# One-megabyte weight loads issued in four pieces, and a list schedule drawn with other ties

## Chip, cores and metric

One core of a Trainium2 chip runs the whole program. The metric is the device time of one execution in microseconds (us); the number given for a kernel is the median of several runs. The kernel before takes 2373.57 us, the median of 3 runs that lie between 2373.34 and 2375.6 us.

## The reference, cut to what matters

One sequence of 2048 tokens with 1024 features goes through four residual layers, A, B, A, B. Both A layers use the same weights, and so do both B layers.

```python
x = A_x                                               # (1, 2048, 1024) bf16
x = x + A(layernorm(x));  x = x + B(layernorm(x))
x = x + A(layernorm(x));  x = x + B(layernorm(x))

A: q, k, v = x @ wqkv                                 # 32 heads of 32
   phi(t) = [softmax(t @ w_phi), softmax(-t @ w_phi)]
   kv = phi(k).T @ v;  z = sum(phi(k))                # 64 x 32 for each head
   return (phi(q) @ kv / (phi(q) . z + 1e-6)) @ wo    # cost linear in the tokens
B: p = softmax(q @ k.T / sqrt(32))                    # 2048 x 2048 for each head
   return (p @ v) @ wo
```

Layer B holds most of the work: 32 heads times 2048 x 2048 exponentials, twice.

## The kernel before, in words

The residual stream `xT` stays in SBUF with the features on partitions (8 feature blocks of 128). Tokens are handled in four chunks of 512. Everything else that lives in SBUF is cut from one large tile, `arena`, and everything in PSUM from one tile, `psum`, of eight banks; so most rows of the profile name only these two.

**Nothing is issued in the order of the source.** Each helper (`layernorm`, `a_keys`, `a_queries`, `b_k`, `b_v`, `b_o`, `attention`, `slab`, ...) only records operations: an engine, a duration that the planner believes, dependencies, buffers, a priority, and a function that emits the instructions. `Sched.run` (line 152) is a list scheduler. It plays the engines forward in its own time, gives each free engine the ready operation with the lowest priority value whose buffers it can allocate, and places the buffers in the arena at that moment. Its result is one order of operations, emitted as it stands; on the chip every engine then works through its own list in order, with semaphore waits where data come from another engine. A small change of a believed duration can therefore move thousands of instructions, though no instruction is added.

The work falls into five stages:

- **A of layer pair 1**: chunks are normalized, keys and values of A are made (`a_keys`, matmuls at line 480, exponentials at L688, softmax sums L692/L695/L701), then queries (`a_queries`, L814 to L883), and A's projection (L896). TensorE works without a break.
- **B of layer pair 1** (`attention`): for each group of three units TensorE makes a score tile of 128 x 1536 (line 1104, three matmuls of 32 rows that run side by side), ScalarE takes its exponential (L1113), and TensorE multiplies the result by the values and by ones (L1145, four matmuls of 32 columns that run side by side). Some units are left to VectorE, which builds 2^x out of integer and polynomial steps (L1047 to L1061, its scores at L1040). Into the gaps of TensorE go the projections for later head groups and chunks (the same helper as at line 480, but in column quarters, so at line 484) and, where nothing is ready, filler matmuls: at L1377 (zeros added to the open accumulator) or through line 484 with `onesD`. The fillers are there to keep TensorE busy enough; the planner puts one in when less than 75% of the last 3.4 us of its own time was worked (`KEEP`, `SPELL`).
- **The change of layers**: the last chunk's output projection, then A of pair 2 for queries, as above. The keys of A for three of four chunks were already made among B's exponentials (`a_keys(..., alone=True)`, with the evictions at L685), and their normalized chunks were stored to DRAM (`xd`, L1368) and are loaded back (L1262).
- **B of layer pair 2**, and **a short tail** (L1171 to L1182, L1022, L1024).

The denominators of B take a round trip: when both accumulators of a head group are copied out (L1161), four small DMAs bring the sums onto more partitions (L1191), VectorE inverts them (L1196), one DMA writes them to DRAM (`rd`, L1197), one reads them back spread over 128 partitions (L1199), and two multiplications finish the group (L1202). All loads and stores but two are issued by the SP queue, one after the other; SP waits for the arena's space before a load, and all that stands behind a load waits too.

Weights come through `slab(cls, prio, src, n)` (line 582). With n = 512 that is a 1 MB load of 128 partitions x 8 feature blocks x 512: the values' and keys' weights of A (`wv_slab`, `wk_slab`, from A_wqkv and from `wd_k`), those of the queries from `wd_q`, B's value weights (`bv_s`) and B's output weights of the last layer (`bo_s`). With n = 128 it is 256 KB (`w2`, `w2o`). A consumer (`mmg2`, line 738) takes the eight blocks in four steps of two, and waits at step i for entry i of the list that `slab` returns; before the change the list holds the same load four times.

Two constants of the planner matter below: a DMA of kb kilobytes costs it 0.55 us on the issuing queue and 2.0 + kb/200 us until it has landed, and `RING` lets half of the size part of one transfer delay the next.

## Time and profile before

| what | value |
|---|---|
| median of 3 runs | 2373.57 us (2373.34 to 2375.6) |
| the profiled execution's own time | 2381.73 us |
| its span, first to last instruction | 2379.9 us |
| mean granted TensorE clock in it | 0.989 |
| ScalarE busy | 2072.2 us, 87% |
| TensorE busy | 2241.8 us, 94% (fillers among it) |
| VectorE busy | 1669.0 us, 70% |
| SP queue | 112.29 MB, 17.6% of 16 DMA engines' time |

The profile is one execution; the chip's profiler records the start and end of each instruction. "Idle before" a group of instructions is the time that its engine stood still just ahead of it, followed by what ended the wait. A row of a table of stretches gives the stretch, its length, the busy time of each engine with the number of instructions, then the granted clock of TensorE (1.00 is full speed), the busy share of the DMA engines and the GB/s.

### The profile page before, as it was taken

Reading aid. Unit: us, or ns where it says so; the run is one execution under the profiler, and the core shown is the slowest. Engines: PE = TensorE matmul, PEld = TensorE weight load, DVE = VectorE, ACT = ScalarE, POOL = GpSimd, SP = SyncE. Lnnn points to the kernel's source line nnn. Section 1 sums busy time; section 2 is a strip of 40 time slices with the busy share of each in tenths; the row PEclk is TensorE's granted clock in tenths of the full one; section 3 lists DMA queues with packets and bytes.
Section 4 is the critical chain, followed back from the end, with each engine's and each line's share of the span. In section 5 each row is a group of like instructions: output and inputs, shape, how many; then the busy total and the mean of one; then the engine's idle time right before and its main releaser. Section 6 shows DMA issues by size and latency. Waiting matters only on the chain.

```text
span 2379.9 us, 67117 instructions
## 1 busy us (share of the span) xinstructions
PE 2241.8 (94%) x29746; PEld 872.4 (37%) x29816; DVE 1669.0 (70%) x2135; ACT 2072.2 (87%) x1850; POOL 25.2 (1%) x70
## 2 busy tenths in 40 slices
PE   7999999999999999999998999999999999899998
PEld 4443343333333333333333434433333333333333
DVE  7987752345678676764764776489888988977763
ACT  5436559999999999999997555899999999999998
POOL 0000000000000000000000000000000000000000
PEclk9999999999999999999999999999999999999999
DMA  9210101122131222213323001110111101111111
GB/s 213 64 37 1 32 21 36 29 52 53 44 92 54 57 59 68 82 55 86 112 73 108 28 3 34 31 27 25 36 27 31 33 25 29 40 50 44 38 30 35
DMA packets 218092, 118.69 MB, mean 50 GB/s; under 512 B 139208, under 2 KB 208840, under 8 KB 217032
## 3 DMA queue, kind: packets, MB, share of 16 engines
q1 hardware_dynamic: 215720, 112.29, 17.6%
q8 instruction: 233, 3.82, 0.7%
q10 hardware_dynamic: 2080, 2.10, 0.3%
q14 instruction: 59, 0.48, 0.1%
HBM read 78.71 MB, written 14.14 MB: 39 GB/s over the span
## 4 chain that ended last, share of the span: by engine, by line
ACT 26%; PE 16%; issue 6%; DVE 5%; DMA 1%; SPq 0%; ACTq 0%; DVEq 0%; another core or an unknown queue 0%
ACT arena L1113 25%; PE psum L480 8%; PE psum L484 2%; PE psum L1145 2%; PE psum L1104 2%; DVE arena L1058 2%; DVE arena L1061 1%; DMA arena<-rd 1%; DVE arena L1047 1%; DVE arena L1050 0%; ACT arena L688 0%; DVE arena L1202 0%; PE psum L857 0%; PE psum L1377 0%; DVE arena L1161 0%
## 5 line engine op out<-in xcount | busy, mean ns | idle before, releaser
L1113 ACT ACTIVATE arena<-psum 128x1536 bf16<-128x1536 f32 x1295 | 1749.4, 1670 | 20.5 <-PE psum L1104 12.9
L1145 PE MATMUL psum<-arena 128*32 128x512 bf16 x4096 | 626.7, 386 | 12.1 <-DVE arena L1161 7.6
L1145 PE MATMUL psum<-arena,ones_bf 128*32 128x512 bf16 x4096 | 626.6, 386 | 1.3 <-issue 1.3
L484 PE MATMUL psum<-arena 128*32 128x512 bf16 (+1 forms) x9792 | 590.0, 356 | 6.5 <-DVE arena L920 3.0
L1104 PE MATMUL psum<-arena 32*128 32x512 bf16 x3884 | 513.9, 384 | 84.0 <-ACT arena L1113 75.0
L480 PE MATMUL psum<-arena 128*128 128x512 bf16 (+1 forms) x1969 | 446.6, 376 | 10.8 <-DVE arena L1182 3.6
L1058 DVE SCALAR_TENSOR_TENSOR arena<-arena 128x1024 f32<-128x1024 f32 x318 | 387.7, 1219 | 6.3 <-PE psum L1145 2.2
L1104 PEld LDWEIGHTS <-arena 32*128 32x128 bf16 x3884 | 173.7, 91 | 572.5 <-issue 561.4
L484 PEld LDWEIGHTS <-arena 128*32 128x32 bf16 x9792 | 221.6, 96 | 231.0 <-issue 120.0
L480 PEld LDWEIGHTS <-arena 128*128 128x128 bf16 x2032 | 190.6, 98 | 245.6 <-issue 45.9
L1145 PEld LDWEIGHTS <-arena 128*32 128x32 bf16 x4096 | 166.8, 95 | 247.1 <-issue 191.1
L1047 DVE TENSOR_SCALAR arena<-psum 128x512 int32<-128x512 f32 x212 | 145.8, 688 | 80.4 <-PE psum L1040 69.6
L920 DVE CAST arena<-psum 128x512 bf16<-128x512 f32 x120 | 82.5, 687 | 155.7 <-PE psum L484 141.7
L1145 PEld LDWEIGHTS <-ones_bf 128*32 128x32 bf16 x4096 | 163.8, 95 | 30.3 <-issue 15.9
L1061 DVE SCALAR_TENSOR_TENSOR arena<-arena 128x1024 bf16<-128x1024 f32 x106 | 129.3, 1220 | 3.5 <-PE psum L1145 0.2
L688 ACT ACTIVATE arena<-psum 128x512 bf16<-128x512 f32 x80 | 43.0, 597 | 87.5 <-PE psum L480 66.6
L1161 DVE COPY arena<-psum 128x512 f32<-128x512 f32 x126 | 86.4, 686 | 44.1 <-PE psum L1145 43.0
L1377 PE MATMUL psum<-xT,zero 128*32 128x512 bf16 x1360 | 111.5, 384 | 0.0
L1202 DVE TENSOR_TENSOR arena<-arena 64x512 bf16<-64x512 f32 x124 | 84.7, 683 | 34.4 <-DMA arena<-rd 21.0
L692 DVE TENSOR_REDUCE arena<-arena 128x32 f32<-128x1024 bf16 x64 | 77.7, 1214 | 32.5 <-ACT arena L688 31.0
L814 ACT ACTIVATE arena<-psum 128x512 bf16<-128x512 f32 x128 | 69.4, 597 | 31.4 <-PE psum L480 30.6
L572 DVE TENSOR_TENSOR arena<-xT,arena 128x1024 f32<-128x1024 bf16 x64 | 77.8, 1219 | 24.4 <-ACT arena L561 23.8
(102 smaller groups left out, 1359.4 us busy)
## 6 DMA issues: line engine op xcount, KB each, us to landing
arena<-rd SPq DMA_DIRECT2D x62, 256.0 KB
arena<-in_B_wqkv_dram SPq DMA_DIRECT2D x48, 256.0 KB
arena<-in_A_wqkv_dram SPq DMA_DIRECT2D x10, 1024.0 KB
arena<-arena SPq DMA_DIRECT2D x256, 32.0 KB
arena<-in_B_wo_dram SPq DMA_DIRECT2D x32, 256.0 KB
arena<-wd_k SPq DMA_DIRECT2D x8, 1024.0 KB
arena<-arena SPq DMA_DIRECT2D x96, 64.0 KB
arena<-in_B_wqkv_dram SPq DMA_DIRECT2D x4, 1024.0 KB
```

Of the source, the lines that this page charges most:

```text
L480: nc.tensor.matmul(out_, lhsT=lhsT, rhs=rhs, start=start, stop=stop, skip_group_check=True)
L484: nc.tensor.matmul(out_[ks, :], lhsT=lhsT[:, ks], rhs=rhs, start=start, stop=stop, tile_position=(0, 32 * k), skip_group_check=True)
L920: return op("DVE", dve_us(512), lambda: nc.vector.tensor_copy(out=dst(), in_=src()), [dep], bufs, prio)
L1047: ys.append(op("DVE", dve_us(512), lambda k=k, s_v=s_v: nc.vector.tensor_scalar(out=y_v()[:, k, :].bitcast(I32), in0=s_v(), scalar1=POW2_B ...
L1058: last = [op("DVE", dve_us(1024), lambda i=i, c=c: nc.vector.scalar_tensor_tensor(out=x_v(), in0=(x_v() if i else m_v()), scalar=c, in1=m_ ...
L1061: eo = op("DVE", dve_us(1024), lambda: nc.vector.scalar_tensor_tensor(out=e_v(), in0=x_v(), scalar=POW2_0, in1=y_v(), op0=ALU.add, op1=ALU ...
L1104: nc.tensor.matmul(out=s_v()[:, x * C512:(x + 1) * C512], lhsT=kT[g][1]()[r, pp, d * P:(d + 1) * P], rhs=q_of[(qc, g)][1]()[r, (pp + j // ...
L1113: ex = op("ACT", act_us(w * C512), lambda s_v=s_v, e_v=e_v, w=w: nc.scalar.activation(out=e_v()[:, 0:w * C512], in_=s_v(), func=ACT.Exp, s ...
L1145: nc.tensor.matmul(out=a_v()[col:col + 32, :], lhsT=v_v()[:, kc % 4, o:o + DH] if what == 0 else ones_bf[:], rhs=ev()[:, x * C512:(x + 1) ...
L1161: cp = op("DVE", dve_us(512), lambda t_v=t_v, a_v=a_v: nc.vector.tensor_copy(out=t_v(), in_=a_v()), [last], [a_b, t_b], prio - 4)
L1202: s = [op("DVE", dve_us(512), lambda a=a, k=k, o_v=o_v, r_v=r_v, T=T: nc.vector.tensor_tensor(out=o_v()[a, :], in0=T[k][1]()[a, :], in1=r_ ...
L1377: nc.tensor.matmul(psum[32 * k:32 * k + 32, 6 * C512:7 * C512], lhsT=zero[:], rhs=xT[:, 0, 0:C512], start=False, stop=False, tile_position ...
```

## The change

Loads with n = 512 are issued as four DMAs of two feature blocks each (256 KB), and the list that the consumer waits on holds the four pieces. The three loads of normalized chunks at L1262 are cut in the same way. Loads with n = 128, the turned loads of `slab_turned` (L595), the two loads on ScalarE's queue (L603) and the three stores at L1368 stay as they are. And before planning, each believed duration of a VectorE or TensorE operation is multiplied by a random factor between 0.99 and 1.01, drawn with seed 14, so that operations that tied or nearly tied are taken in another order.

```diff
+TIE = 14
 ...
     def run(self):
+        draw = random.Random(TIE)
+        for o in self.ops:
+            if TIE and o.eng in ("DVE", "PE"):
+                o.dur *= 1 + draw.uniform(-0.01, 0.01)
 ...
     def slab(cls, prio, src, n, deps=(), q="SP"):
         b, v = sb(cls, PO, n)
-        o = dma(prio, lambda: (nc.sync if q == "SP" else nc.scalar).dma_start(out=v(), in_=src),
-                deps, [b], q=q, kb=2 * n)
-        return b, v, [o] * 4
+        if n < C512:
+            o = dma(prio, lambda: (nc.sync if q == "SP" else nc.scalar).dma_start(out=v(), in_=src),
+                    deps, [b], q=q, kb=2 * n)
+            return b, v, [o] * 4
+        return b, v, [dma(prio + 0.001 * i, lambda i=i: (nc.sync if q == "SP" else nc.scalar).dma_start(
+            out=v()[:, 2 * i:2 * i + 2, :], in_=src[:, 2 * i:2 * i + 2, :]),
+            deps, [b], q=q, kb=n / 2) for i in range(4)]
 ...
-                xnA[c] = (x_b, x_v, [dma(second - 20 + 20 * c, lambda c=c, x_v=x_v: nc.sync.dma_start(
-                    out=x_v(), in_=xd_v[:, c, :, :]), [xnA[c]], [x_b], kb=1024)] * 4)
+                xnA[c] = (x_b, x_v, [dma(second - 20 + 20 * c + 0.001 * i, lambda c=c, x_v=x_v, i=i: nc.sync.dma_start(
+                    out=x_v()[:, 2 * i:2 * i + 2, :], in_=xd_v[:, c, 2 * i:2 * i + 2, :]),
+                    [xnA[c]], [x_b], kb=256) for i in range(4)])
```

More of the change, by code (lines that the diff above doesn't have):

```diff
@@ L2 @@
 import math
+import random
 from contextlib import ExitStack
```

## Prediction

> **What bounds the kernel now.** I read the busy times by stage first, cut where the first and the last exponential of each attention lie; the first attention begins at 357.5. A row is stretch, length, then PE, PEld, DVE, ACT and POOL busy with their instructions.

> ```profile
> 357.50:1285.00 927.50, 872.26 (x13218) 321.10 (x13219) 557.00 (x705) 911.78 (x712) 11.51 (x24) 0.99 0.23 65
> 1285.00:1499.70 214.70, 209.99 (x1556) 89.67 (x1575) 154.62 (x213) 117.65 (x201) 2.60 (x8) 0.98 0.10 30
> 1499.70:2369.00 869.30, 815.85 (x12020) 305.88 (x12022) 679.75 (x837) 860.78 (x645) 0.00 (x0) 0.99 0.12 33
> ```

> TensorE bounds the change of layers (second row). In the two attentions ScalarE does: it is idle for 927.50 - 911.78 = 15.7 us of the first and 869.30 - 860.78 = 8.5 us of the second. So an order that only moves work inside the attentions can win at most 24 us. Next, the groups by line, to see who waits there:

> ```profile
> L1113 ACT ACTIVATE arena<-psum 128x1536 bf16<-128x1536 f32 x1295 | 1749.4, 1670 | 20.5 <-PE psum L1104 12.9 <-PE psum L484 3.7 <-PE psum L1145 2.8
> ...
> L484 PEld LDWEIGHTS <-arena 128*32 128x32 bf16 x9792 | 221.6, 96 | 231.0 <-issue 120.0 <-DMA arena<-in_B_wqkv_dram 0.8 <-DVE arena L576 0.3
> ```

> The exponentials waited 20.5 us in all, for TensorE. The second row has the largest wait of these projections for a weight load, 0.8 us. Where do the 20.5 us lie? In stretches of 10 us with a low granted clock (third number from the end), one undisturbed stretch first:

> ```profile
> 1020.00:1030.00 10.00, 8.68 (x117) 2.97 (x118) 9.86 (x13) 10.00 (x8) 0.53 (x1) 1.00 0.03 8
> 1090.00:1100.00 10.00, 7.54 (x200) 2.77 (x192) 0.83 (x2) 6.92 (x6) 0.00 (x0) 0.83 0.42 124
> 1180.00:1190.00 10.00, 9.50 (x119) 3.19 (x119) 8.02 (x8) 6.26 (x7) 0.09 (x1) 0.79 0.09 25
> 1210.00:1220.00 10.00, 8.83 (x80) 2.31 (x79) 7.94 (x12) 8.14 (x7) 0.59 (x1) 0.66 0.01 3
> 1270.00:1280.00 10.00, 8.01 (x94) 2.31 (x91) 6.40 (x9) 7.62 (x6) 0.00 (x0) 0.83 0.25 54
> 1700.00:1710.00 10.00, 10.00 (x119) 2.88 (x115) 7.84 (x10) 9.00 (x7) 0.00 (x0) 0.85 0.06 15
> 1750.00:1760.00 10.00, 8.45 (x96) 2.56 (x95) 9.04 (x12) 9.16 (x7) 0.00 (x0) 0.83 0.01 1
> 1810.00:1820.00 10.00, 9.83 (x123) 2.83 (x119) 8.26 (x10) 8.89 (x7) 0.00 (x0) 0.89 0.06 15
> 1970.00:1980.00 10.00, 10.00 (x122) 2.90 (x119) 8.81 (x10) 9.21 (x8) 0.00 (x0) 0.87 0.05 12
> ```

> ScalarE loses 10 minus its fourth busy time: 3.08, 3.74, 1.86, 2.38, then 1.00, 0.84, 1.11 and 0.79 us, 14.8 together. These **falls of the clock** are what an order can change. What comes ahead of one, in single us:

> ```profile
> 1175.00:1176.00 1.00, 0.39 (x3) 0.10 (x3) 1.00 (x2) 1.00 (x1) 0.00 (x0) 1.00 0.33 113
> 1176.00:1177.00 1.00, 0.45 (x4) 0.19 (x4) 1.00 (x3) 1.00 (x2) 0.00 (x0) 1.00 0.09 33
> 1178.00:1179.00 1.00, 1.00 (x11) 0.30 (x12) 0.87 (x2) 1.00 (x2) 0.00 (x0) 0.50 0.05 4
> ```

> Two us with TensorE below half busy, then half clock. Such a gap can be found in the program's order: I counted the matmuls that stand between one score group (L1104 x3) and the next. In five places of the attentions (their starts aside) two neighbouring intervals hold five matmuls or fewer. By the number of the exponential they stand at 486, 589, 801, 880 and 998, and the counts of exponentials up to a time place them (the fourth, 880, lies between the last two rows):

> ```profile
> 0.00:1026.00 1026.00, 658.53 (x487) 1.00 0.23 58
> 0.00:1176.90 1176.90, 797.31 (x589) 1.00 0.24 63
> 0.00:1698.00 1698.00, 1084.13 (x801) 0.99 0.21 56
> 0.00:1968.00 1968.00, 1350.47 (x999) 0.99 0.20 52
> ```

> The last four, where one interval is empty and the other holds five, are each followed by one of the falls above (1180, 1700, 1810, 1970). The first, with four matmuls and then one, is not (1020 to 1030 has clock 1.00). The other four falls do not stand in the order: they come from waits as they happened.

> **The change part by part.** *Loads in pieces.* 26 loads and the three of L1262 become four DMAs each, 87 issues more on SP. An earlier first piece is worth what waits for a load now; that is about 0.8 us by the row above, and taken as 0 (bounds 0 and -0.8). Issues cost most at the start, where SP has no pause:

> ```profile
> 13.82 1.04 SPq L584 DMA_DIRECT2D arena<-in_A_wqkv_dram  x2
> ...
> 37.88 7.66 SPq L515 DMA_TRANSPOSE xT<-in_A_x_dram  x3
> ```

> One issue is 1.04/2 = 0.52 us; six more are 3.1 us. In the new order five transposed loads of x stand behind the second store of `wd_k` and not three; that store waits for VectorE, so they end 2 x 7.66/3 = 5.1 us later, at 45.5 + 5.1 = 50.6 us. The first reader of chunk 2 is

> ```profile
> 54.27 3.71 ACT L538 ACTIVATE arena<-xT 128x2048 bf16<-128x2048 bf16 x2
> ```

> so 3.6 us of cover are left: cost 0, and up to 5.1 us if landing takes longer than that.

> [...]

> *The other order.* Instruction counts stay the same on ScalarE and VectorE; TensorE loses 28 filler groups of L1377 (1360 to 1248 matmuls) and gains one of the other kind. The split alone leaves the second attention's TensorE order untouched; the tie seed moves it. Term by term:

> 1. *Falls.* In the new order the sparse places are 762 (four matmuls, then one, like 486 which did not fall) and 998 (five and none, as before). 589, 801 and 880 are filled. That removes 3.74 + 1.00 + 1.11 = 5.85 us. For 762 I add 0.4 of the mean of the three falls of the second attention, 0.4 x (1.00 + 1.11 + 0.79)/3 = 0.39. Bounds: nothing removed and a fall at 762, +0.97; all gone with 998 too, -6.6.

> [...]

> 2. *Start of the second attention.*

> ```profile
> 1499.76 1.45 ACT L1113 ACTIVATE arena<-psum 128x1536 bf16<-128x1536 f32 x1 [0.95 <-PE psum L1104]
> 1501.11 0.71 ACT L564 ACTIVATE arena<-arena,eps 128x512 f32<-128x512 f32 x1
> 1501.86 0.63 ACT L566 ACTIVATE arena<-arena 128x512 f32<-128x512 f32 x1
> ...
> 1513.55 0.37 ACT L919 CAST arena<-psum 128x256 bf16<-128x256 f32 x1 [0.92 <-PE psum L480]
> ...
> 1516.98 13.54 ACT L1113 ACTIVATE arena<-psum 128x1536 bf16<-128x1536 f32 x10 [1.31 <-PE psum L1104]
> ```

> Today the ninth exponential starts at 1516.98, after evictions that TensorE feeds one by one. In the new order ScalarE does L564, L566 and one eviction (L919) first (1501.11 + 0.71 + 0.63 + 0.37 = 1502.8), then six exponentials, two evictions, two exponentials, two evictions: 8 x 13.54/10 + 0.55 + 3 x 0.37 = 12.5, ninth at 1515.3, with one eviction (0.37) still to come. Gain 1516.98 - 1515.3 - 0.37 = 1.3. Bounds: -3.2 (all waits in these rows), +1.9.

> 3. *End of the first attention.* There VectorE stands in L1202 for a round trip of the denominators:

> ```profile
> 1269.67 1.41 DVE L1202 TENSOR_TENSOR arena<-arena 64x512 bf16<-64x512 f32 x2 [4.37 <-DMA arena<-rd]
> ```
> ```profile
> L990 DVE TENSOR_TENSOR arena<-xT,psum 128x512 f32<-128x512 bf16 x8 | 5.5, 688 | 16.7 <-PE psum L484 16.6
> ```
> ```profile
> 1270.43 2.79 ACT L1113 ACTIVATE arena<-psum 128x1536 bf16<-128x1536 f32 x2 [0.75 <-PE psum L1104]
> 1274.19 1.45 ACT L1113 ACTIVATE arena<-psum 128x1536 bf16<-128x1536 f32 x1 [0.97 <-PE psum L1104]
> 1276.62 8.16 ACT L1113 ACTIVATE arena<-psum 128x1536 bf16<-128x1536 f32 x6 [0.97 <-PE psum L1104]
> ```

> Behind it waits the eviction L990, behind that TensorE (one PSUM bank serves these projections), behind that the scores; ScalarE loses 0.75 + 0.97 + 0.97 = 2.69. In the new order three of the eight L990 stand behind L1202 and not one. I take two L990 more, 2 x 0.69 = +1.4 (the second row gives 688 ns for one). Bounds -2.69 and 4.37 - 0.75 = +3.6.

> 4. *Change of layers and tail*: the same matmuls in a TensorE stage 98% busy (209.99 of 214.70): 0, bounds ±2.

> Sum: -5.85 + 0.39 - 1.3 + 1.4 = -5.4 us. The profiled execution took 2381.73, so 2376.3 in its terms; it lies 8.2 us above the median of the runs, and the same difference taken from the median gives 2373.57 - 5.4 = **2368.2 us**, -0.23%.

> **The rivals.**

> *More falls go than the order shows.* The four that come from waits (3.08, 1.86, 2.38, 0.84) are accidents of one order; should the new one avoid those of 1090 and 1210 as well, it is -5.4 - 4.9: 2363.3 us. For: these waits lie among the keys that are made alone, and every one of those moved. Against: the new order has 28 filler groups fewer to cover gaps.

> *No net gain.* Falls return elsewhere, as five of the former eight places did not follow from the order alone (four waits and the phase of the one that stayed harmless at 486): 2373.6 us.

> *Slower: evictions stuck behind the round trips.* VectorE waited 21.0 us for `rd` in 11 of its L1202 places, and only the one at 1269 reached ScalarE:

> ```profile
> DVE arena L1202 <- DMA arena<-rd: 21.0, 11, 4.4
> ```

> SP now puts four issues where one was, 3 x 0.52 = 1.6 us longer ahead of a round trip's next DMA, and the seed places L1202 anew among the evictions. Each further place that reaches the scores costs what that one does, 2.69 us. It decides from (5.4 + 4.7)/2.69, about four places; with five, 2368.2 + 13.4 = 2381.6 us. Against it: few loads are cut inside the second attention.

> [...]

> *The pieces don't do what they say* (nobody waits for a whole load): already in the sum, at 0.

> **How the numbers follow.** A measurement of this kernel tells about 0.2% (4.7 us) from no change, so faster is below 2368.8 and slower above 2378.3. Chances: the forecast 0.42, its own range 2364 to 2373, 0.28 of it below 2368.8; more falls gone 0.17; no net gain 0.12; late start 0.05, 0.04 of it inside; stuck evictions 0.24. Faster 0.28 + 0.17 = 0.45; same 0.14 + 0.12 + 0.04 = 0.30; slower 0.24 + 0.01 = 0.25. The range of 8 in 10: below, the second case with another 4 us (the remaining accidents): 2359; above, the slower case at five places: 2382.

> **What would show it.** Right: clock 1.00 after exponentials 589, 801 and 880 and a fall after 998; ScalarE idle in the attentions below 20 us; the ninth exponential of the second attention about 15 us after the first scores; ScalarE squaring chunk 2 without a wait for x. Wrong: clock falls at places that the order does not mark; L1202 with long waits for `rd` and idle scores behind it; a wait for DMA on TensorE or ScalarE in the first 60 us.

## The result, and the profile after

The changed kernel takes 2370.64 us, the median of 12 runs (2365.42 to 2376.02), beside 2374.03 us for the kernel before on the same chip (12 runs, 2369.76 to 2378.05). The ratio is 0.9983, with a 95% interval of 0.9976 to 0.9991. On another chip it was run once more (after_again below): 0.9987, 0.9975 to 0.9999. So it is faster by 0.1 to 0.2%, 3 to 4 us. Forecast were 5.4 us.

The profiled execution after took 2372.59 us (span 2370.8), close to its median; that of before, 2381.73, lay 7.7 us above its own. The difference of the two profiles, 9.1 us, is therefore mostly one of two executions. Where a place is compared below, more than one profile of an order is used.

The three stages, cut as in the prediction at the first and the last exponentials (stretch, length, busy PE, PEld, DVE, ACT, POOL, then clock, DMA share, GB/s), and the exponentials' group:

```profile
351.50:1277.05 925.55, 868.82 (x13201) 319.03 (x13201) 556.64 (x705) 915.41 (x716) 12.01 (x24) 0.99 0.24 65
1277.05:1491.30 214.25, 209.56 (x1564) 89.31 (x1587) 156.66 (x216) 118.17 (x203) 2.57 (x8) 0.99 0.11 33
1491.30:2359.70 868.40, 810.49 (x11933) 302.67 (x11935) 677.26 (x833) 858.93 (x643) 0.00 (x0) 0.99 0.12 33
```
```profile
L1123 ACT ACTIVATE arena<-psum 128x1536 bf16<-128x1536 f32 x1295 | 1749.7, 1703 | 18.4 <-PE psum L1155 7.3
```

ScalarE's idle time is 10.1 us in the first attention (925.55 - 915.41) and 9.5 in the second (868.40 - 858.93); before it was 15.7 and 8.5. (The prediction's first row begins at 357.5, but the first exponential of before is at 353.30; ScalarE was busy for all of the 4.2 us between, so the 15.7 us stand, and the row's length is not to be compared.) The exponentials (now line 1123) waited 18.4 us in place of 20.5. The change of layers is 0.45 us shorter.

Now the places that the prediction named. Exponentials 589, 801 and 880 lie in the first, third and fourth row of this table of 10 us stretches, 998 in the last two; row two is where the clock fell before behind 589:

```profile
1170.00:1180.00 10.00, 8.71 (x129) 3.14 (x125) 5.20 (x8) 10.00 (x11) 0.32 (x1) 1.00 0.67 220
1180.00:1190.00 10.00, 9.50 (x145) 3.58 (x143) 5.06 (x7) 10.00 (x10) 0.33 (x1) 1.00 0.72 234
1680.00:1690.00 10.00, 9.12 (x117) 2.90 (x112) 8.87 (x13) 10.00 (x9) 0.00 (x0) 1.00 0.03 5
1790.00:1800.00 10.00, 8.72 (x122) 2.85 (x114) 9.94 (x12) 10.00 (x9) 0.00 (x0) 1.00 0.07 15
1950.00:1960.00 10.00, 8.75 (x111) 2.81 (x107) 9.32 (x13) 10.00 (x8) 0.00 (x0) 0.92 0.07 15
1960.00:1970.00 10.00, 9.81 (x122) 2.89 (x114) 8.07 (x10) 8.89 (x8) 0.00 (x0) 0.91 0.06 15
```

The clock stays at 1.00 where the places were filled, ScalarE is busy for the whole 10 us, and 998 falls, as forecast. What the forecast did not have:

```profile
1080.00:1090.00 10.00, 6.45 (x68) 1.79 (x64) 3.19 (x4) 6.65 (x6) 0.00 (x0) 0.73 0.36 74
1090.00:1100.00 10.00, 9.31 (x237) 3.46 (x229) 1.12 (x2) 8.40 (x7) 0.00 (x0) 0.93 0.33 82
...
1860.00:1870.00 10.00, 8.91 (x138) 3.53 (x138) 8.41 (x10) 9.23 (x7) 0.00 (x0) 0.83 0.01 2
...
2080.00:2090.00 10.00, 9.12 (x115) 2.70 (x118) 9.59 (x13) 7.24 (x6) 0.00 (x0) 0.83 0.01 2
```

ScalarE loses 3.35 and 1.60 us at 1080 to 1100 (3.08 before, at 1090), 0.77 us at 1860, where the clock falls at a place that the forecast's count does not mark, and 2.76 us at 2080, where before had a full stretch:

```profile
2080.00:2090.00 10.00, 8.70 (x119) 3.09 (x112) 9.36 (x13) 10.00 (x9) 0.00 (x0) 1.00 0.82 219
```

The cause at 2080 is read from four views of the same microseconds: VectorE, TensorE and ScalarE with the idle time ahead of each group in brackets, and what SP issued.

```profile
2075.11 1.21 DVE L1071 SCALAR_TENSOR_TENSOR arena<-arena 128x1024 bf16<-128x1024 f32 x1
2079.54 0.68 DVE L1212 TENSOR_TENSOR arena<-arena 64x512 bf16<-64x512 f32 x1 [3.22 <-DMA arena<-rd]
2080.15 0.68 DVE L1057 TENSOR_SCALAR arena<-psum 128x512 int32<-128x512 f32 x1
```
```profile
2080.88 0.40 PE L490 MATMUL psum<-xT,onesD 128*32 128x512 bf16 x4 [2.48 <-DVE arena L1057]
```
```profile
2082.76 2.80 ACT L1123 ACTIVATE arena<-psum 128x1536 bf16<-128x1536 f32 x2 [2.46 <-PE psum L1155]
```
```profile
2068.23 0.34 SPq L1207 DMA_DIRECT2D rd<-arena  x1
2068.61 1.46 SPq L594 DMA_DIRECT2D arena<-in_B_wo_dram  x3
2070.11 2.52 SPq L591 DMA_DIRECT2D arena<-in_B_wqkv_dram  x2
2073.04 1.83 SPq L1209 DMA_DIRECT2D arena<-rd  x1
```

The chain runs upward. SP writes a group's denominators (L1207) and, ahead of reading them back (L1209), issues five loads, three of them pieces. VectorE stands 3.22 us in L1212 until the read has landed. Behind L1212 waits L1057, behind that a filler matmul of TensorE that wants L1057's PSUM bank, and behind the filler the scores: ScalarE loses 2.46 us, and 0.23 more at the half clock that follows. Together 2.69 us, the price that the rival "stuck behind the round trips" was given, at one place.

### The profile page after: what moved, and what is told of

It reads as the page before. It is cut to its first block, busy times and chain, and to the rows that moved or that the text cites. A ratio compares the mean times of both kernels' runs of the same rounds, so it can differ in the third digit from the quotient of the medians.

```text
span 2370.8 us, 67055 instructions
## 1 busy us (share of the span) xinstructions
PE 2228.1 (94%) x29641; PEld 864.8 (36%) x29708; DVE 1668.6 (70%) x2135; ACT 2069.9 (87%) x1850; POOL 25.6 (1%) x70
## 3 DMA queue, kind: packets, MB, share of 16 engines
q10 hardware_dynamic: 2080, 2.10, 0.3%
## 5 line engine op out<-in xcount | busy, mean ns | idle before, releaser
L1123 ACT ACTIVATE arena<-psum 128x1536 bf16<-128x1536 f32 x1295 | 1749.7, 1703 | 18.4 <-PE psum L1155 7.3
L1057 DVE TENSOR_SCALAR arena<-psum 128x512 int32<-128x512 f32 x212 | 145.7, 687 | 82.6 <-PE psum L1050 73.1
L1212 DVE TENSOR_TENSOR arena<-arena 64x512 bf16<-64x512 f32 x124 | 84.7, 683 | 39.2 <-DMA arena<-rd 34.2
L1388 PE MATMUL psum<-xT,zero 128*32 128x512 bf16 x1248 | 102.2, 382 | 0.0
```

The lines of the kernel that those rows point to most:

```text
L1057: ys.append(op("DVE", dve_us(512), lambda k=k, s_v=s_v: nc.vector.tensor_scalar(out=y_v()[:, k, :].bitcast(I32), in0=s_v(), scalar1=POW2_B ...
L1123: ex = op("ACT", act_us(w * C512), lambda s_v=s_v, e_v=e_v, w=w: nc.scalar.activation(out=e_v()[:, 0:w * C512], in_=s_v(), func=ACT.Exp, s ...
L1212: s = [op("DVE", dve_us(512), lambda a=a, k=k, o_v=o_v, r_v=r_v, T=T: nc.vector.tensor_tensor(out=o_v()[a, :], in0=T[k][1]()[a, :], in1=r_ ...
L1388: nc.tensor.matmul(psum[32 * k:32 * k + 32, 6 * C512:7 * C512], lhsT=zero[:], rhs=xT[:, 0, 0:C512], start=False, stop=False, tile_position ...
```

## The experiments

The first four ran together on one chip, the next four on one, the last three on one. The kernel before took 2379.63, 2379.27 and 2378.37 us there, so the ratios are compared, not the times.

**1. The order without the pieces (order_whole).** Every engine but SP keeps the changed kernel's instructions one for one.

```diff
-        lambda i=i: (...).dma_start(out=v()[:, 2 * i:2 * i + 2, :], in_=src[:, 2 * i:2 * i + 2, :])
+        lambda i=i: i == 0 and (...).dma_start(out=v(), in_=src)
```

> The order of the changed kernel on every engine but SP, with each one-megabyte load issued whole where its first piece stood. If the gain comes from the order (my theory), it keeps the gain: 2369 to 2372 us, about 2370.6. If it comes from the pieces (first rival), it is back at 2374. If the pieces cost something because four issues hold up the reads of the denominators behind them (second rival; in the profile after, the reads at 1074 and 2073 stand behind pieces and VectorE waits 3.7 and 3.2 us for them), it is faster than the changed kernel by up to 5 us: 2366.

Measured: 0.9972 (0.9957 to 0.9987). The whole gain is there without a single piece on the chip; what the pieces changed in the plan is still in it, since the order was planned with them. The second rival is not borne out by its own place: with whole loads the waits at the same two round trips remain, 2.45 us of ScalarE's time at 1081 and 2.08 at 2077, and VectorE's sum of waits for `rd` is no smaller. One row of VectorE's waits each (total us, times, longest), of the changed kernel and of this one:

```profile
DVE arena L1212 <- DMA arena<-rd: 34.2, 15, 7.4
```
```profile
DVE arena L1212 <- DMA arena<-rd: 36.0, 16, 7.7
```

**2. The pieces without the order (before_pieces).** The kernel before, each 1 MB load emitted as four DMAs at its place.

```diff
-        o = dma(prio, lambda: (...).dma_start(out=v(), in_=src), deps, [b], q=q, kb=2 * n)
+        o = dma(prio, lambda: [(...).dma_start(out=v()[:, r:r + 2, :], in_=src[:, r:r + 2, :])
+                               for r in range(0, 8, 2)] if n == C512 else ..., deps, [b], q=q, kb=2 * n)
```

> The order of the kernel before on every engine, only the 29 one-megabyte loads issued as four pieces at the place where the whole load stood. If only the order matters: 2374 us, within 2 us of before. If the pieces bring the gain: 2370.6. If the pieces hold up the denominators: above 2375, with more than 21 us of waits for rd at L1202's multiplications.

Measured: 0.9992 (0.9979 to 1.0005): the pieces by themselves change nothing that can be told. This profile is also a second look at the order of before:

```profile
1180.00:1190.00 10.00, 8.90 (x134) 3.28 (x135) 9.17 (x10) 8.62 (x8) 0.00 (x0) 1.00 0.28 79
1690.00:1700.00 10.00, 8.75 (x99) 2.80 (x100) 8.41 (x10) 8.93 (x7) 0.00 (x0) 0.83 0.01 2
1800.00:1810.00 10.00, 8.74 (x99) 2.65 (x100) 9.01 (x11) 8.91 (x7) 0.00 (x0) 0.83 0.06 14
1960.00:1970.00 10.00, 8.69 (x96) 2.49 (x88) 9.32 (x11) 9.22 (x8) 0.00 (x0) 0.83 0.07 16
```
```profile
DVE arena L1204 <- DMA arena<-rd: 32.3, 14, 4.9
```
```profile
56.02 3.71 ACT L538 ACTIVATE arena<-xT 128x2048 bf16<-128x2048 bf16 x2
```

801, 880 and 998 fall again; 589 does not, and costs 1.38 us in place of 3.74. VectorE's waits for `rd` are 11.3 us longer than the 21.0 of before, as the extra issues on SP would have it, and hardly any of that reaches ScalarE. The first reader of x's second chunk is 1.75 us later than the 54.27 of before: with the old order the issues at the start do show, in this one profile. In the new order it begins at 53.70 with pieces (trips_again) and at 53.61 without (order_whole), the clock being full ahead of it in both; so there they cost 0.1 us, in the main as forecast. (54.32 in the changed kernel's own profile stands behind one step of half clock.)

**3. Filling the sparse places (after_dbl).** Where little TensorE work stands between two score groups, the first group is computed again into the same banks, 293 repeats in all.

```diff
-    for o in sch.run():
-        o.fn()
+    plan = sch.run()
 ...                                                    # between: us of TensorE work up to the next score group
+            o.again = 2 if between < 0.3 else 1 if between < 0.55 else 0
+    for o in plan:
+        for _ in range(1 + o.again):
+            o.fn()
```

> The changed kernel, with a score group computed once or twice again (the same values into the same banks) where fewer than 0.55 or 0.3 us of other TensorE work stand before the next score group in the plan. If falls of the clock come from sparse places of the order, those at 1862 and 1958 go and the mean clock rises to 0.995 or more; falls stay only behind waits of 2.5 us and more (1082, 1263, 2080); the time falls by 2 to 4 us, to 2367 to 2369. If such falls cost nothing that is not hidden, it stays at 2370.6. If the repeated scores hold up the exponentials, it is slower than 2372, with more idle time before the exponentials and no fewer falls.

Measured: 1.0001 (0.9989 to 1.0014). The falls at 1862 and 1958 are gone, the clock is 0.996, and the gain with them:

```profile
1950.00:1960.00 10.00, 9.98 (x131) 3.25 (x131) 9.92 (x14) 10.00 (x8) 0.00 (x0) 1.00 0.12 33
1960.00:1970.00 10.00, 9.34 (x128) 2.98 (x125) 8.95 (x11) 10.00 (x9) 0.00 (x0) 1.00 0.05 11
...
1860.00:1870.00 10.00, 9.45 (x122) 3.05 (x123) 9.07 (x12) 10.00 (x8) 0.00 (x0) 1.00 0.21 48
```
```profile
L1125 ACT ACTIVATE arena<-psum 128x1536 bf16<-128x1536 f32 x1295 | 1750.4, 1604 | 23.2 <-PE psum L1115 9.7
```

That fits falls made by sparse places, though it is one profile, and 998 stayed at full clock without any repeats in one of eight (trips_again). The forecast of 2 to 4 us gained failed: the exponentials now wait 23.2 us, 9.7 of them for their scores, in place of 18.4 and 6.3. That the repeats stand in the way of scores that were only just in time fits the row; which of the 293 do it wasn't separated.

**4. Reads of the denominators first (after_rdfirst, after_trips).** The planned order is kept; the loads (the turned ones apart) that SP issues between a group's write L1207 and its read L1209 go behind the read. First in all 62 round trips:

```diff
+    for bk in [o for o in plan if o.back is not None]:      # bk: the read; bk.back: its write
+        lo, hi = plan.index(bk.back), plan.index(bk)
+        late = [o for o in plan[lo + 1:hi] if o.load and not any(x in plan[lo:hi] for x in o.out)]
+        plan[lo + 1:hi + 1] = [o for o in plan[lo + 1:hi + 1] if o not in late] + late
```

> The changed kernel, with the weight loads that SP issues between the write and the read-back of one group's denominators moved behind the read. If those pieces are what makes the read late, the waits at 1082 and 2080 (ScalarE idle 2.5 us each) shrink below 0.5 us and the time falls by 3 to 6 us, to about 2366; the waits of the L1212 multiplications for rd fall from 34 to about 20 us. If the read is late because of transfers already on the queues, nothing changes: 2370.6. If the loads come too late instead, TensorE waits for DMA and it is slower.

Measured: 0.9963 (0.995 to 0.9976). The stall at 1082 is gone, that at 2080 is 1.23 us, but VectorE's sum of waits for `rd` is 32.7 us, not 20. I then took waits of this profile at 400, 818 and 959 for the price of the other moves, and moved loads in two trips alone:

```diff
-    for bk in [o for o in plan if o.back is not None]:
+    for bk in [o for o in plan if o.back is not None][24:52:27]:     # the 25th and the 52nd
```

> The changed kernel; only in the two round trips whose read stood behind loads and held up the scores (the 25th and the 52nd of the 62) the read goes ahead of these loads (four pieces of A's values' weights; three of B's output weights and two small ones). If the read was late because of these loads, ScalarE's 2.5 us at 1082 and 2.5 us at 2080 go, with the half clock behind them (another 1 to 2 us): 4 to 6 us less than the changed kernel beside it, and none of the new waits at 400, 818 and 959 that moving all loads brought. If the read is late without them too, no difference beyond 1 us.

Measured: 0.9960 (0.9948 to 0.9972), and 0.9953 (0.9936 to 0.9969) when it was run again (trips_again). On the chip of after_again it is 6.6 us faster than the changed kernel (2367.96 against 2374.6), and the fastest version of the study that was run twice. In the two profiles the two places account for 3.3 us of that (4.52 to 0.76 us of ScalarE's idle time at the first, 1.29 to 1.73 at the second); where the rest lies is open. Here are SP's queue and VectorE at the 25th trip, the changed kernel first, then this one (its line numbers lie one to eight further on):

```profile
1071.35 0.34 SPq L1207 DMA_DIRECT2D rd<-arena  x1
1071.78 2.52 SPq L594 DMA_DIRECT2D arena<-in_A_wqkv_dram  x4
1074.48 0.59 SPq L1209 DMA_DIRECT2D arena<-rd  x1
```
```profile
1082.85 1.40 DVE L1212 TENSOR_TENSOR arena<-arena 64x512 bf16<-64x512 f32 x2 [3.68 <-DMA arena<-rd]
```
```profile
1072.84 0.34 SPq L1214 DMA_DIRECT2D rd<-arena  x1
1075.51 0.58 SPq L1216 DMA_DIRECT2D arena<-rd  x1
1076.14 2.24 SPq L595 DMA_DIRECT2D arena<-in_A_wqkv_dram  x4
```
```profile
1081.43 1.41 DVE L1220 TENSOR_TENSOR arena<-arena 64x512 bf16<-64x512 f32 x2 [0.76 <-DMA arena<-rd]
```

The read is issued 3.13 us after the write with the loads between and 2.67 without; that is not much. But VectorE can go on 8.4 us after the issue (1074.48 to 1082.85) with 1 MB ahead of it in the queues, and 5.9 us (1075.51 to 1081.43) without. The other profiles agree: with 1 MB ahead 8.7 us in after_again and 8.8 in order_whole, without it 6.0 to 6.5 in after_rdfirst, trips3, trips_again and trips3_whole. In order_whole the megabyte is one single issue and the read is issued 2.67 us after its write, as in after_trips, and yet VectorE goes on at 1082.01, 8.8 us after the issue at 1073.24. So it is the transfer ahead that makes the read late, not the number of issues, and this is why whole loads (experiment 1) do no better. The stall at 2080 shrank only to 1.73 us; the read there still comes 4.3 us after its write, though SP has nothing between them. The waits at 400 and 959 are absent here, but one at 400 (2.25 us) is back in trips3, where nothing ahead of it was moved, and one at 954 (3.05 us) in after_again; so these two are no price of the other moves, and my reason for leaving those out doesn't hold. The wait at 818 (2.4 us with what follows) came back in no other run; whether it is a price of the moves is open.

**5. A third trip, and whole loads again (trips3, trips3_whole, trips_again).** The 31st trip, at the end of the first attention, stands behind turned pieces of A's output weights, which now count as loads too.

```diff
-    for bk in [o for o in plan if o.back is not None][24:52:27]:
+    for bk in [[o for o in plan if o.back is not None][n] for n in (24, 30, 51)]:
```

> As after_trips, and in a third round trip too (the 31st, at the end of the first attention) the read goes ahead of the loads that stood before it (three turned pieces of A's output weights and one small load). If the waits there come from the late read as in the other two, ScalarE's 2.6 us at 1260 to 1265 fall to below 1 us, and with the half clock at 1262 and 1276 the kernel is 1.5 to 4 us faster than trips_again beside it. If not (the same chain through one PSUM bank, whatever the read does), within 1 us of it.

> As trips3, with each one-megabyte load issued whole where its first piece stood. If four issues cost nothing here, within 0.1% of trips3 (2 us). If the pieces still cost SP time or the queues something, it is 1 to 3 us faster than trips3, as order_whole (0.9972) stood to the changed kernel (0.9983 and 0.9987). If pieces are what makes the first readers early, it is slower.

> after_trips once more, beside trips3 on the same chip: 0.996 of before, within 0.9948 to 0.9972.

Measured: trips3 0.9954 (0.9936 to 0.9971), the same as trips_again's 0.9953: no gain in the third place, where VectorE still waits:

```profile
1264.05 1.41 DVE L1221 TENSOR_TENSOR arena<-arena 64x512 bf16<-64x512 f32 x2 [2.88 <-DMA arena<-rd]
```

trips3_whole: 0.9967 (0.9955 to 0.998). Whole loads are 0.13% behind the pieces here, 0.11 and 0.15% ahead of them in experiment 1, and 0.08% behind in experiment 2; the intervals overlap each time. The sign changes with the order, and the pieces as such come out at nothing, within about 0.15%. At one place the profiles do show a difference. At 2080 ScalarE loses 3.58 us in trips3_whole and nothing in trips3: two whole loads (2 MB) stand ahead of the write there and not five pieces, and the read is issued 7.24 us after the write (2064.44 to 2071.68) and not 3.96 (2067.90 to 2071.86).

**6. The pieces planned without the seed (split_t0), another seed (split_t10), the change again (after_again).** The first is one part of the change alone: `TIE = 0`; the second has `TIE = 10`.

> The changed kernel once more, for a second profile and on the chip of the runs beside it. Theory: the clock is granted in fixed steps of 3.413 us that run from a phase of their own in each execution, so the places that are only just too sparse (950, 1859, 1955) fall in some executions and not in others, and those with TensorE idle for over 2.5 us (1082, 1263, 2080) fall each time. Expected: the starts of all falls lie whole multiples of 3.413 us apart; 0.9983 of before again, within 0.9972 to 0.9995. Rival: the falls belong to the order alone, then they are at the same eight places.

> The loads in pieces as in the change, planned without the random factor (one part of the change alone). The order has empty places at exponentials 801, 880 and 998 as before, and 486 with none in its second interval. By my forecast's rule it keeps the falls of the second attention and is within 0.1% of before: 0.999 to 1.001, about 3 to 4 us slower than the changed kernel. Rival: the pieces in the plan bring the gain, then it is at 0.998 like the change.

> The changed kernel with seed 10 in place of 14, a layout whose order has no place with five matmuls or fewer in two neighbouring intervals. By the forecast's rule the falls at sparse places are gone, that at 998 too (1.1 us), so it is 1 us faster than the changed kernel, 0.9979 of before. Rival: what decides is where VectorE stands in L1212 for the denominators' round trip, and that is a lottery of each layout: then it differs from the changed kernel by as much as 3 to 5 us either way, whatever the count of sparse places says.

Measured: after_again 0.9987 (0.9975 to 0.9999). Its falls in the attentions start at 955, 1091, 1228 and 1958, those of the first profile at 1085, 1265, 1498, 1863, 1958 and 2081: the same program, other places, as the theory of steps has it. What I expected of the stalls held for 1082 alone; those at 1263 and 2080 were only 0.84 and 1.29 us long this time, and did not fall.

split_t0 0.9970 (0.9959 to 0.9981), split_t10 0.9983 (0.997 to 0.9996). The expectation for split_t0 (0.999 to 1.001) failed; that for split_t10 (0.9979) lies in the interval, as does no difference from the changed kernel. The layout without the seed still has its empty places. Of those in the second attention two fall, and that at 486, with four matmuls and none, falls too, at 1023:

```profile
1690.00:1700.00 10.00, 8.75 (x111) 2.83 (x107) 9.76 (x12) 10.00 (x9) 0.00 (x0) 1.00 0.01 0
1800.00:1810.00 10.00, 9.76 (x114) 2.84 (x113) 8.76 (x10) 9.19 (x8) 0.00 (x0) 0.83 0.05 10
1960.00:1970.00 10.00, 8.91 (x102) 2.55 (x101) 7.74 (x10) 9.07 (x8) 0.00 (x0) 0.83 0.07 15
```

Yet it is no slower than the changed kernel. Its profile has neither of the two stalls (1082, 2080): ScalarE's longest wait in its attentions is 2.25 us, at 1265. And seed 10, with no sparse place at all, is where seed 14 is; its longest waits are 3.12 us at 1264 and 2.34 at 942. The count of sparse places does not order the layouts; the few places where a wait of VectorE comes through to the scores weigh as much in these profiles. What makes split_t0 0.2% faster than before_pieces, which has the same second attention on TensorE, isn't settled: their two profiled executions differ by 1.4 us alone.

This bears on the largest term of the forecast. The seed is what fills 801 and 880, and in the runs side by side the plan with the seed was no faster than the one without (medians 2374.60 and 2372.54 us; the intervals just overlap). The mean clock of all timed runs, which does not hang on one profile, says the same: 0.9923 in before (35 runs), 0.9928 in after_again, 0.9949 in split_t0 (12 each), all on one chip. In the profiles below the filled places are won, and about as much is lost at the two round trips; why a new plan is faster at all is shown only in part.

## Why the prediction was right, and where it was not

The time lies in the range and on the side that was forecast, and the order and not the pieces brings the gain (0.9972 without pieces, 0.9992 without the order, though the interval of the latter, down to 0.9979, leaves room for a part of it). Of the prediction's signs, those of being right all came: full clock at 589, 801 and 880, a fall at 998, less than 20 us of idle time, no wait for x. But two of its three signs of being wrong came too: falls at places that the order does not mark, and idle scores behind L1212. Term by term it was right at the filled places, missed two round trips, and met the total in part by luck.

ScalarE's idle time in us at the places of the sum, added up from its waits over 0.15 us, in two profiles of the order of before and three of the order after:

| place | before | before_pieces | after | after_again | order_whole |
|---|---|---|---|---|---|
| exponentials 589, 801, 880 | 5.84 | 3.47 | 0 | 0 | 0 |
| 762 | 0 | 0 | 0 | 0 | 0 |
| 998 | 0.78 | 0.78 | 1.10 | 1.08 | 1.08 |
| start of the second attention | 3.23 | 3.24 | 3.70 | 1.69 | 1.69 |
| end of the first | 2.69 | 2.66 | 2.35 | 1.06 | 2.38 |
| round trip at 1082, to 1101 (before: at 1095) | 3.08 | 1.92 | 5.13 | 4.52 | 5.28 |
| round trip at 2080 | 0 | 0 | 2.69 | 1.29 | 2.08 |
| both attentions, all places | 22.6 | 17.7 | 19.1 | 17.5 | 15.5 |

*Term 1, the falls (-5.85 and +0.39).* The mechanism is right: the places fall when sparse and not when filled. Of the places with five matmuls and none, 801, 880 and 998 fell in eight of nine cases in the three profiles with the old second attention, and 998 in seven of the eight profiles that have the new order without the repeats of experiment 3. 762, with four and one, fell in none of these eight (its emptiest step has a matmul under way for 0.76 of the time in the three of the table above), so the +0.39 was not needed. The size was that of one execution: the second profile gives 3.47, so the mean removed is 4.7 us. (589 shows it best: TensorE has the same matmuls there in both profiles, and ScalarE waits 3.74 us where the clock fell and 1.31 where it did not.)

*Term 2, the start of the second attention (-1.3).* Right: 3.2 us became 1.69 in two profiles; in the third a fall at 1497 took it to 3.70. The ninth exponential begins 13.9, 13.9 and 16.4 us after the first, against 17.2 before.

*Term 3, the end of the first attention (+1.4).* Wrong in sign, by 1.7 to 3.0 us: a loss of 1.4 was forecast, and 0.3 to 1.6 were won. More evictions (now L1000) follow the wait, but TensorE waits for the first alone, 2.26 us at 1265, its only wait for L1000 in the whole profile. To count evictions that nobody waits for was the error.

*The pieces (0).* Right, within about 0.15%, by experiments 1, 2 and 5. One reading behind it was too wide: that about 0.8 us is what waits for a load in before holds for the loads that are cut; TensorE waited 10.0 us in two waits at the very start for A's weights, which come on ScalarE's queue and are left whole, and 9.5 us after the change. The late start (5.1 us, chance 0.05) did not come: x's second chunk is first read at 54.32 us in the changed kernel and at 53.70 in trips_again, beside 54.27 in before.

No run shows in the time what three more DMAs cost a load that is cut. Where a load's size did matter, it was the megabyte ahead of the 256 KB read of `rd` in the queues, and at 1082 one piece or four make little difference: VectorE goes on 8.8 us after the read's issue with one (order_whole) and 8.4 and 8.7 us with four (the changed kernel, after_again), against 5.9 to 6.5 us with no megabyte ahead.

*The rival that was partly true.* Not about four places of stuck evictions, as it would have taken to lose, but two: 2080 is new, and 1082 costs 5 us where the order before lost 2 to 3 us close by, at 1095, to a pause of TensorE. Experiment 4 takes the first away, and gains 0.27% beside after_again, more than the whole change. I had given the mechanism its price and left its number to chance, though the order on SP (which loads stand between a group's write and read) and VectorE's order (what stands behind L1212) can both be read before a run.

The sum, by the means of the table: 4.7 us won at the filled places, 0.9 at the start and 0.7 at the end; lost 2.5 at 1082, 2.0 at 2080 and 0.3 at 998. That is 1.5 us won; over all places of the two attentions it is 2.8 (20.2 to 17.3), so 1.3 us lie at places that no term named. The first stage, where the forecast had 0, ends at 350.7 to 352.4 us in the eight profiles of the new order without repeats, against 353.3 in before and 355.3 in before_pieces. Part of that is luck: the new order's end goes with the steps of half clock in the first 30 us (350.7 to 350.8 with none, 351.5 to 351.6 with one, 352.2 to 352.4 with two), and before had two. At two steps each, 1 us is won, and no run shows by what. Together that is in the region of the 3 to 4 us measured; two and three executions don't tell it finer. The forecast of -5.4 came as close as it did because a missed loss of 4.5 us met gains that it had not counted: that part is luck.

## What to carry to other kernels

Before a change of order is priced by its largest group, list what each engine's queue holds behind every wait for a DMA round trip, and what stands on the issuing queue between the two halves of that trip; moving the loads at two such places gained more here than the change. A list schedule drawn anew is a draw: price the places that can be read from the order, and leave the rest in the range. And a profile is one execution: with half-clock steps that come and go, two profiles of one order differed by 5 us in ScalarE's idle time.

## What the runs showed of the hardware

| share of the step with a matmul | steps | next at half clock |
|---|---|---|
| below 0.50 | 35 | 35 |
| 0.50 to 0.60 | 26 | 13 |
| 0.60 to 0.65 | 58 | 18 |
| 0.65 to 0.75 | 229 | 5 |
| 0.75 and more | 8308 | 0 |

This replaces the prediction's "Two us with TensorE below half busy". A stall of 3 us puts at least 1.5 us of idle time into one step wherever the grid lies, so that step is at 0.56 or below, and of the 61 steps below 0.60 48 were followed by a fall. The sparse place at 998 shows what the phase does. In ten profiles one step holds the whole place, stands at 0.617 to 0.646, and a fall follows each time; in trips_again the grid cuts the place into steps of 0.91 and 0.72, and none follows. But the share doesn't decide alone: 801 in split_t0, at 0.633, is not followed by a fall. (The shares rest on modelled ends of matmuls; between 0.5 and 0.7 both outcomes stand side by side, for that reason or another.) Little idle time was enough at times: steps with 1.2 to 1.4 us of it, the third row, were followed by a fall in 18 of 58 cases.

**The scatter goes with the clock.** Among the 12 timed runs of the changed kernel the fastest, 2365.42 us, had a mean clock of 0.996, and two of 2376.0 had 0.990 and 0.992. The records of before and after show the clock at 1.00 or at 0.50 and at nothing between, so a mean of 0.990 is 2 x 0.010 x 2374 = 47 us at half clock, 0.996 is 19 us: 28 us more of it, 10.6 us of time. Over the 12 runs time and clock are correlated at -0.79, over the two sets of 35 runs of before at -0.80 and -0.87. Whether the phase makes the difference or waits that lower the clock isn't shown by these runs.
